# Block attention with a top-1 MoE on one core: six router operations as scalar_tensor_tensor, and a new order of steps in nine plan strings

## The chip, the cores and the metric

The kernel runs on one core of a Trainium2 chip. Its time is the device time of one execution in microseconds; the median of three runs before the change is 945.31 us (942.5 to 946.25). The engines are TensorE (PE, with its weight loads shown apart as PEld), VectorE (DVE), ScalarE (ACT), GpSimd (POOL) and SyncE (SP, which here only issues DMAs).

## What is computed

Attention over 8 batches of 8 heads, 576 positions of 64 values, where a query sees the blocks of 64 keys up to its own; then its output, 4608 tokens of 512 values, goes through a mixture of 8 experts of which each token takes one.

```python
def _attn_ref(q, k, v):
    scores = scale * np.matmul(q, k.transpose(0, 1, 3, 2))
    mask = block_i >= block_j                     # blocks of 64
    scores = np.where(mask, scores, -1000000000.0)
    scores = scores - np.max(scores, axis=-1, keepdims=True)
    attn = np.exp(scores)
    attn = attn / (np.sum(attn, axis=-1, keepdims=True) + 1e-09)
    return np.matmul(attn, v)

def _moe_ref(x, expert_emb, tau, w1, w2):
    xn = x / (np.linalg.norm(x, axis=-1, keepdims=True) + 1e-06)
    en = expert_emb / (np.linalg.norm(expert_emb, axis=-1, keepdims=True) + 1e-06)
    logits = xn @ en.T / tau
    expert_idx = np.argmax(logits, axis=1)
    probs = np.exp(logits - logits.max(-1, keepdims=True))
    probs /= probs.sum(-1, keepdims=True) + 1e-09
    gate_w = probs[np.arange(N), expert_idx]
    for e in range(E):                            # 512 -> 1024 -> 512
        h = np.maximum(x[expert_idx == e] @ w1[e], 0.0)
        out[expert_idx == e] = gate_w[...] * (h @ w2[e])
```

## The kernel before

**Attention.** A loop of 32 iterations, n = 0 to 31, handles one pair of heads each: batch b = n // 4, pair n % 4. An iteration works on four pairs at once, in stages: the scores of n, the row maxima of n+1, the transposes and casts of n+2, the values and the finish of n-1, and the loads of n+3. Each stage is a Python generator that writes its instructions up to a `yield`, one step at a time. A **plan string** says which generator takes its next step, letter by letter, and so sets the order in which every engine's queue is written:

- `s`, scores(n), 10 steps of which five belong to each head: two matmuls on PE (L366 and L367, of 288, 288, 448, 320, and 192 + 64 columns), the exponential on ACT (L376, L383), and for the last three of five an addition to the row sums' tile pS on POOL (L357, `add`).
- `m`, maxes(n+1), 12 steps: 11 with a matmul (L336) into psm (two buffers) and a reduction on DVE (L337), then one that turns the maxima (L342), copies them on ACT (nmT, L344) and sends them with two SP DMAs to qx.
- `v`, values(n-1), 9 steps: six of value matmuls on PE (L396) into psb, a copy of them on ACT (oe, L402), the row sums and the router's products on PE (L411, L414) into the same psb, and their copy on ACT (su, L416).
- `f`, finish(n-1), 4 steps: transposes of su and oe on PE into psb (L426, L428); the reciprocals and the scaled rows on DVE (L433 to L437); the router's logits on DVE (L440, L443); the end, at which the fourth pair of a batch puts that batch's router on the list `slow`.
- `p`, prep(n+2), 6 steps: transposes of q and k on PE (L295), casts on ACT (L307, L311, L316), low parts on DVE (L286), copies within SBUF by SP DMAs (L309, L319).
- `l`, the loads of n+3: seven SP DMAs.
- `r`, one step of the oldest router on `slow`, nothing when there is none. The router of a batch, route(b), is some 45 small operations on DVE, five squares on ACT, a power on POOL (L538), ranks on PE into psm (L496 to L500), the store of the rows, and five scatters into a table in DRAM, which are indirect DMAs issued by POOL (L560). The last router but one ends with `early_rows`: index arithmetic on POOL (L576 to L580) and two gathers (L591) of tokens for the first expert.
- `k`, in iteration 0 alone, a part of the router's set-up.

PLAN0 is for n = 0, the first four strings of PLANS for n % 4 = 0, 1, 2, 3, and the last four for n = 28 to 31. Letters that are missing are drained at the iteration's end. psb has one buffer, so finish(n-1) waits for ACT's copy of the sums, and values(n) in the next iteration wait for the last read of finish(n-1) on DVE (L443). An engine runs its queue in the order written, and waits where an operand isn't there.

**After the loop** the list `slow` is drained, the first expert's weights are split into high and low parts (L741, L745), the two gathered tiles are turned on PE (L927), the values, the finish and the router of the last pair run between the first expert matmuls (L940), and the other slots follow one after another to the end.

Of the kernel before, what the change touches and what calls it, by code (L numbers as in the profile page):

```python
# [8 lines left out]
F32 = mybir.dt.float32  # L9
# [4 lines left out]
ALU = mybir.AluOpType  # L14
# [16 lines left out]
PLAN0 = "smkmmmskspmmmrmmsmpkrspmsssslpspp"


@with_exitstack
def kernel(
# [30 lines left out]
    const = ctx.enter_context(tc.tile_pool(name="const", bufs=1))  # L66
# [96 lines left out]
    def pool(stack, name, bufs, **kw):  # L163
        return stack.enter_context(tc.tile_pool(name=name, bufs=bufs, **kw))
# [8 lines left out]
    op = pool(left, "op", 1)  # L173
# [290 lines left out]
    def bc(ap, *shape):  # L464
        return ap.to_broadcast(shape)

    def route(b, xrow, lgh, ssp):

        lg = sm.tile([P, NJ, E], F32, name="lg")
# [5 lines left out]
        nc.vector.tensor_scalar(lg, lg, itau, None, op0=ALU.mult)
# [32 lines left out]
        nc.vector.tensor_tensor(acc, acc, oa, op=ALU.add)
        yield
        if b == B - 1:  # L510
            nc.vector.tensor_tensor(accb, acc, early, op=ALU.subtract)
        else:
            nc.vector.tensor_copy(accb, acc)
# [16 lines left out]
        ss = sm.tile([P, NJ], F32, name="ss")  # L530
        gs = sm.tile([P, NJ], F32, name="gs")
# [10 lines left out]
        nc.vector.tensor_scalar(ss, ss, 1.0e-6, None, op0=ALU.add)
# [3 lines left out]
        nc.vector.tensor_tensor(lg, lg, bc(ss.unsqueeze(2), P, NJ, E), op=ALU.mult)
# [149 lines left out]
    for n in range(NPAIR):  # L696
# [613 lines left out]
```

## Time and profile before

| | |
|---|---|
| median of three runs | 945.31 us |
| the profiled execution | 943.41 us |
| its span | 941.6 us |
| mean granted clock of TensorE | 0.964 |
| attention's loop, from the first value matmul to the end of n = 31 | 34.1 to about 466 us |
| a batch (four iterations), n = 5 to 8 | 55.1 us |
| a batch, n = 21 to 24 | 58.0 us |

A row of the timeline reads: start in us, duration, engine, line, operation, output<-inputs with their shapes, xcount where equal neighbours are drawn together, and in brackets how long the engine stood before it and what ended that. A row of the windows reads: stretch and width, busy time of PE, PEld, DVE, ACT and POOL with the number of instructions, then the granted clock, the share of the DMA engines, and GB/s. A row of a group by lines ends with its total and the mean in ns, then the idle time before.

### The profile page before, as it was taken

To read this page: it belongs to the slowest core of one execution; us is meant where nothing else is said; L and a number is where in the kernel's file an instruction comes from. 1 tells how busy PE (TensorE), PEld (TensorE's weight loads), DVE (VectorE), ACT (ScalarE), POOL (GpSimd) and SP (SyncE) were. 2 spreads that over 40 slices of the span, in tenths; PEclk is the share of its full clock that TensorE was granted. 3 is DMA by queue.
4 is the path that set the end of the run, shared out by engine and by line. 5 is a ranking of instruction groups with operands and counts; after the bars stand their busy time and mean duration, and the time that the engine had idled before them with its cause. 6 is when DMAs were issued, how large, how long until landed. Compare 5 with 4: busy or idle time off the path is not lost. (4 is left out here: it accounts for less than half of the span.)

```text
span 941.6 us, 20617 instructions
## 1 busy us (share of the span) xinstructions
PE 878.1 (93%) x5609; PEld 673.8 (72%) x5609; DVE 681.6 (72%) x1602; ACT 486.9 (52%) x1028; POOL 447.2 (47%) x483
## 2 busy tenths in 40 slices
PE   5999989898998989998688999999999999999997
PEld 4676666667666666666466788777888888888886
DVE  7577868686785867757377488767777888888882
ACT  3565757476575755746555453545444332253222
POOL 5344554646454463544743074687747211173111
PEclk9999999999997989979789899999999999999999
DMA  7766867576684756845345444464535211111111
GB/s 148 158 140 142 197 129 154 138 150 158 139 197 105 158 138 129 200 104 165 126 171 186 176 146 136 136 203 143 185 101 185 85 47 47 47 43 47 47 42 45
DMA packets 155175, 122.29 MB, mean 130 GB/s; under 512 B 122217, under 2 KB 123513, under 8 KB 155020
## 3 DMA queue, kind: packets, MB, share of 16 engines
q1 hardware_dynamic: 147372, 100.14, 42.9%
q0 software_dynamic: 7648, 20.44, 6.8%
q8 instruction: 54, 0.88, 0.4%
q14 instruction: 101, 0.83, 0.3%
HBM read 72.71 MB, written 19.71 MB: 98 GB/s over the span
## 5 line engine op out<-in xcount | busy, mean ns | idle before, releaser
L986 DVE STREAM_TRANSPOSE pt<-h 32x256 f32<-32x256 f32 x528 | 240.8, 456 | 18.5 <-ACT h L958 0.5
L337 DVE TENSOR_REDUCE nmx<-psm 128x1 f32<-128x320 f32 x315 | 136.8, 454 | 88.3 <-PE psm L336 76.6
L376 ACT ACTIVATE pT<-pss 128x448 f32<-128x448 f32 (+1 forms) x254 | 110.1, 452 | 103.0 <-PE pss L367 95.6
L745 POOL TENSOR_TENSOR ring_l<-raw,ring_h 128x1024 f32 (+1 forms) x52 | 123.7, 2408 | 41.1 <-ACT ring_h L741 40.3
L357 POOL TENSOR_TENSOR pS<-pS,pT 128x320 f32<-128x320 f32 (+2 forms) x192 | 115.3, 600 | 54.1 <-ACT pT L376 25.8
L357 POOL TENSOR_TENSOR pS<-pT 128x448 f32<-128x448 f32 x64 | 73.0, 1140 | 142.8 <-ACT pT L376 142.7
L366 PE MATMUL pss<-qb,ka 128*128 128x448 f32 (+1 forms) x382 | 129.0, 349 | 7.6 <-ACT pT L376 4.7
L1000 POOL DMA_INDIRECT out_dram<-y,outi x36 | 36.0, 1001 | 197.7 <-ACTq L894 142.3
L336 PE MATMUL psm<-kd,qd 128*128 128x320 f32 x315 | 105.2, 368 | 18.9 <-DVE nmx L337 12.3
L367 PE MATMUL pss<-qx,kx 70*128 70x448 f32 (+1 forms) x382 | 115.2, 322 | 3.4 <-DMA qx<-nmT 2.2
L940 PE MATMUL py<-ring_h,hh 128*128 (+1 forms) x280 | 113.0, 404 | 2.6 <-ACT hh L992 2.6
L396 PE MATMUL psb<-pT,vo 128*64 128x64 f32 (+4 forms) x768 | 113.9, 422 | 0.0
L940 PE MATMUL py<-ring_h,hl 128*128 (+1 forms) x280 | 112.1, 400 | 1.1 <-DVE hl L994 1.0
L940 PE MATMUL ph<-ring_h,xh 128*128 x280 | 110.3, 394 | 0.5 <-issue 0.5
L940 PE MATMUL ph<-ring_l,xh 128*128 x280 | 110.0, 393 | 0.5 <-POOLq L906 0.5
L940 PE MATMUL ph<-ring_h,xl 128*128 x280 | 110.0, 393 | 0.0
L940 PE MATMUL py<-ring_l,hh 128*128 (+1 forms) x280 | 109.8, 392 | 0.0
L336 PEld LDWEIGHTS psm<-kd,qd 128*128 128x128 f32 x315 | 59.2, 199 | 65.1 <-DVE nmx L337 36.0
L366 PEld LDWEIGHTS pss<-qb,ka 128*128 128x128 f32 x382 | 78.2, 205 | 26.2 <-ACT pT L376 10.9
L958 ACT ACTIVATE h<-ph 128x512 f32<-128x512 f32 x70 | 41.9, 599 | 93.6 <-DVE pt L986 74.8
L994 DVE TENSOR_TENSOR hl<-pt,hh 128x512 fp32r<-128x512 f32 x66 | 42.5, 686 | 63.7 <-ACT hh L992 61.5
L367 PEld LDWEIGHTS pss<-qx,kx 70*128 70x128 f32 x382 | 79.0, 207 | 5.1 <-issue 4.1
(262 smaller groups left out, 1578.9 us busy)
## 6 DMA issues: line engine op xcount, KB each, us to landing
raw<-in_moe_w_dram SPq DMA_DIRECT2D x64, 512.0 KB
ka<-kd SPq DMA_DIRECT2D x128, 144.0 KB
qn<-in_q_dram SPq DMA_DIRECT2D x64, 144.0 KB
kn<-in_k_dram SPq DMA_DIRECT2D x64, 144.0 KB
qx<-qb SPq DMA_DIRECT2D x32, 288.0 KB
vo<-in_v_dram SPq DMA_DIRECT2D x64, 128.0 KB
xbuf<-xrow SPq DMA_DIRECT2D x7, 1040.0 KB
qx<-nmT SPq DMA_DIRECT2D x64, 2.2 KB
```

The lines of the kernel that those rows point to most:

```text
L336: nc.tensor.matmul(mx[:, 0:e - a], qd[d][:, j, :, :], kd[d][:, a:e], start=True, stop=True)
L337: nc.vector.tensor_reduce(m[:, j + u:j + u + 1], mx[:, 0:e - a], axis=AX.X, op=ALU.max, negate=True)
L357: nc.gpsimd.tensor_tensor(o, pT[0:r, P:S] if t == 1 else o, pT[0:r, off[t]:off[t] + w], op=ALU.add)
L366: nc.tensor.matmul(o, ka[i][:, hh, ts], qb[i][:, hh, c0:c1], start=True, stop=False)
L367: nc.tensor.matmul(o, kx[i][0:KX, hh, ts], qx[i][0:KX, hh, c0:c1], start=False, stop=True)
L376: nc.scalar.activation(pT[:, o:o + c1 - c0], st[:, 0:c1 - c0], AF.Exp, scale=scale)
L396: nc.tensor.matmul(ob[hh * D:(hh + 1) * D, c0:c1], a[:, t, hh, :], pTs[hh][0][:, o:o + c1 - c0], start=(t == 0), stop=(c0 == 448 or t == N ...
L745: return eng.tensor_tensor(piece(ring_l, to, c, half), raw[i][:, c * CW:(c + 1) * CW], piece(ring_h, to, c, half).bitcast(F32), op=ALU.sub ...
L940: m = nc.tensor.matmul(out, ac, w, start=(c == 0 and w is wh and a is sh), stop=(c == nk - 1 and a is sl_))
L958: nc.scalar.activation(h[:, f:f + 512], ph, AF.Relu)
L986: nc.vector.transpose(pt[32 * j:32 * j + 32, :, 32 * i:32 * i + 32], h[32 * i:32 * i + 32, :, j, :])
L994: nc.vector.tensor_tensor(sets["hl"][u], pt[:, 4 * u:4 * u + 4], sets["hh"][u].bitcast(F32), op=ALU.subtract)
```

## The change

Six DVE operations of the router become scalar_tensor_tensor, four of them with a new tile of zeros, zeroj, or a slice of it as the second tensor; each computes what it computed. zeroj is one more memset ahead of the loop. All nine plan strings are written anew; the letters of the stages are the same in number, but for `r`, of which many now fall where no router is pending and do nothing. Lines behind L121 move by two, so L357 before is L359 after.

```diff
 PLANS = (
-    "rrrvvsmmrvmsrrvmsvrvvmrmpmrrsvvrprsmrsrlmrrmfrrmmrpfsfrpssrfsrrprp",
-    "mvrvrvvmrmrvmvsmmvssrpsmsrrvrvssprpmmfmlsfmfprfrmsrpsrp",
-    "mrrvvrrrmvmmvvvmvmsspmssvrvrlrpsmsrmmfpffrmsspfrspmrrprsrrrr",
-    "rvvrrrrrvvrmrrsmrrrsrmrspmmvvrvrrsrmmprvrmmrrrrvrssmfmrrprsmrrlfrsprrsrsfprrfp",
+    "rrrrrvrrvrvvvvmsmsvmrrmsrsrmrrprrrrmsmrrrsrrrmvrrrrrrrvrsrsrprrrpmrrmfrrrrrrfrrrrrrrrmlfrrfsprsrrrprmp",
+    "vvvvvvmrsmsrvmsmsmpmsmsrmvvpspmsmfmflprfrmprrrrsrsrfp",
+    "vvvvvvvmssmrmsmpmsmsvvpmmssmmfpmsrflfmrrppsrpsf",
+    "rvvrvssmrmrsrsrrmrpmrvvvvprmmrrrvvmsmpsmfrrrrrmfffsrsmlpsrrsmrrpprr",
...
-    "rrvrrvrrvvrmrrsmrsrrrrmrspmmvmrvrrsrmvprvrrrmmrvrssmfmrprsmrrfrslprsrsrfrrfpp",
+    "vlmrvmrvprrrpvvmvpvmspsmmrmrmvmrrrmmvssprpfsfsfmfssss",
 )
...
+    zeroj = const.tile([P, NJ, E], F32, name="zeroj")
+    nc.vector.memset(zeroj, 0.0)
...
-        nc.vector.tensor_scalar(lg, lg, itau, None, op0=ALU.mult)
+        nc.vector.scalar_tensor_tensor(lg, lg, itau, zeroj, op0=ALU.mult, op1=ALU.add)
...
-        nc.vector.tensor_tensor(acc, acc, oa, op=ALU.add)
+        nc.vector.scalar_tensor_tensor(acc, oa, 1.0, acc, op0=ALU.mult, op1=ALU.add)
...
-            nc.vector.tensor_copy(accb, acc)
+            nc.vector.scalar_tensor_tensor(accb, acc, 1.0, zeroj[:, 0], op0=ALU.mult, op1=ALU.add)
...
-        nc.vector.tensor_scalar(ss, ss, 1.0e-6, None, op0=ALU.add)
+        nc.vector.scalar_tensor_tensor(ss, ss, 1.0e-6, zeroj[:, :, 0], op0=ALU.add, op1=ALU.add)
...
-        nc.vector.tensor_tensor(lg, lg, bc(ss.unsqueeze(2), P, NJ, E), op=ALU.mult)
+        nc.vector.scalar_tensor_tensor(lg, lg, 1.0, bc(ss.unsqueeze(2), P, NJ, E), op0=ALU.mult, op1=ALU.mult)
...
-        nc.vector.tensor_scalar(gs, gs, 1.0e-9, None, op0=ALU.add)
+        nc.vector.scalar_tensor_tensor(gs, gs, 1.0e-9, zeroj[:, :, 0], op0=ALU.add, op1=ALU.add)
```

Where the order changes, three places are shown. The first is POOL's queue around the five scatters of a batch; L357 (L359 after) is the addition to pS, in the sizes 448, 320, 192 and 64 for each head of a pair. Before:

```order
L357 TENSOR_TENSOR pS<-pT 128x448
L357 TENSOR_TENSOR pS<-pS,pT 128x320
L357 TENSOR_TENSOR pS<-pS,pT 128x192
L357 TENSOR_TENSOR pS<-pS,pT 64x64
L560 DMA table<-tokf,rowj 36864x1 x5
L357 TENSOR_TENSOR pS<-pT 128x448
```

The five scatters stood together between two iterations' additions. After, at the same place of a batch, in iteration n % 4 = 3:

```order
L359 TENSOR_TENSOR pS<-pT 128x448
L359 TENSOR_TENSOR pS<-pS,pT 128x320
L562 DMA table<-tokf,rowj 36864x1
L359 TENSOR_TENSOR pS<-pS,pT 128x192
L359 TENSOR_TENSOR pS<-pS,pT 64x64
L562 DMA table<-tokf,rowj 36864x1 x4
L359 TENSOR_TENSOR pS<-pT 128x448
```

The scatters moved behind the first head's additions, the first of them ahead of the last two.

The second place is PE from the transposes of a finish to the first value matmul of the next iteration, at the end of n = 4 (n % 4 = 0). psb is the shared buffer, L342 turns the maxima, L295 transposes k, L366 and L367 are scores. Before:

```order
L428 MATMUL psb<-ident,oe_194 128x128 x5
L342 MATMUL psm<-ident,nmx_192 9x128
L366 MATMUL pss<-qb_176,ka_182 128x288
L367 MATMUL pss<-qx_179,kx_185 128x288
L295 MATMUL pst<-ident,kn 128x96 x6
L366 MATMUL pss<-qb_176,ka_182 128x448
L367 MATMUL pss<-qx_179,kx_185 128x448
L366 MATMUL pss<-qb_176,ka_182 128x320
L367 MATMUL pss<-qx_179,kx_185 128x320
L366 MATMUL pss<-qb_176,ka_182 128x192
L367 MATMUL pss<-qx_179,kx_185 128x192
L366 MATMUL pss<-qb_176,ka_182 128x64
```

One more score matmul and one of maxima followed, then the first value matmul. After, from the same transposes on:

```order
L344 MATMUL psm<-ident,nmx_194 9x128
L368 MATMUL pss<-qb_178,ka_184 128x320
L369 MATMUL pss<-qx_181,kx_187 128x320
L297 MATMUL pst<-ident,kn 128x96 x6
L368 MATMUL pss<-qb_178,ka_184 128x192
L369 MATMUL pss<-qx_181,kx_187 128x192
L368 MATMUL pss<-qb_178,ka_184 128x64
L369 MATMUL pss<-qx_181,kx_187 128x64
L398 MATMUL psb<-pT,vo_161 64x64 x2
L398 MATMUL psb<-pT,vo_161 64x512 x2
L398 MATMUL psb<-pT,vo_161 64x448 x2
L398 MATMUL psb<-pT,vo_161 64x320 x2
```

The score steps of 288 and 448 columns and the maxima no longer stand between, and the value steps follow each other, six in a row, before the first of the maxima.

The third place is POOL at the end of the loop, n = 31, around the two gathers ex. Before:

```order
L357 TENSOR_TENSOR pS<-pT 128x448
L357 TENSOR_TENSOR pS<-pS,pT 128x320
L576 CAST ei<-et 128x2
...
L580 CAST ei<-enone 128x2
L591 DMA ex_202<-xbuf,ei 128x520
L591 DMA ex_203<-xbuf,ei 128x520
L357 TENSOR_TENSOR pS<-pS,pT 128x192
L357 TENSOR_TENSOR pS<-pS,pT 64x64
L357 TENSOR_TENSOR pS<-pT 128x448
L357 TENSOR_TENSOR pS<-pS,pT 128x320
```

Two further additions followed. After, all eight additions stand ahead:

```order
L359 TENSOR_TENSOR pS<-pT 128x448
L359 TENSOR_TENSOR pS<-pS,pT 128x320
L359 TENSOR_TENSOR pS<-pS,pT 128x192
L359 TENSOR_TENSOR pS<-pS,pT 64x64
L578 CAST ei<-et 128x2
...
L582 CAST ei<-enone 128x2
L593 DMA ex_204<-xbuf,ei 128x520
L593 DMA ex_205<-xbuf,ei 128x520
L747 TENSOR_TENSOR ring_l_6399<-raw_124,ring_h_6398 128x1024
```

The gathers moved behind the last six additions of the loop, and behind them POOL goes on with the weights' low parts.

More of the change, by code (lines that the diff above doesn't have):

```diff
@@ L21 @@
 PLANS = (
-    "rrrvvsmmrvmsrrvmsvrvvmrmpmrrsvvrprsmrsrlmrrmfrrmmrpfsfrpssrfsrrprp",
-    "mvrvrvvmrmrvmvsmmvssrpsmsrrvrvssprpmmfmlsfmfprfrmsrpsrp",
-    "mrrvvrrrmvmmvvvmvmsspmssvrvrlrpsmsrmmfpffrmsspfrspmrrprsrrrr",
-    "rvvrrrrrvvrmrrsmrrrsrmrspmmvvrvrrsrmmprvrmmrrrrvrssmfmrrprsmrrlfrsprrsrsfprrfp",
-    "rrrvvmsmrvmsrrvmmsvrvvmrpmrrrsvvprsmrsrlrrmmfrrmmrpfspfsrsrfsrrprp",
-    "rmvvrvrvvvmvmmrsmmssrpsmsrrrvvssprpmmfmlsfmfprsfrmprsrp",
-    "mmvrrrvvrmvssprmmvvmvmssvrvrmrlrpsmsmfpffrmsrspsfrpmrrprsrrrr",
-    "rrvrrvrrvvrmrrsmrsrrrrmrspmmvmrvrrsrmvprvrrrmmrvrssmfmrprsmrrfrslprsrsrfrrfpp",
+    "rrrrrvrrvrvvvvmsmsvmrrmsrsrmrrprrrrmsmrrrsrrrmvrrrrrrrvrsrsrprrrpmrrmfrrrrrrfrrrrrrrrmlfrrfsprsrrrprmp",
+    "vvvvvvmrsmsrvmsmsmpmsmsrmvvpspmsmfmflprfrmprrrrsrsrfp",
+    "vvvvvvvmssmrmsmpmsmsvvpmmssmmfpmsrflfmrrppsrpsf",
+    "rvvrvssmrmrsrsrrmrpmrvvvvprmmrrrvvmsmpsmfrrrrrmfffsrsmlpsrrsmrrpprr",
+    "vvvvrvvmmssmrvmsrsrmpmsmsrmvvrpsprmsmfmflffrppssmrp",
+    "vvvrvmrmrssmsmsmrpmrmvrvvmsspmmvprvmsrrlspmrfrsfsfppf",
+    "rrmprrrspvvrvvmmsrsvrmmsrsmmlmvvsrmsmrrvvrprprsspfsmrffrrprfmr",
+    "vlmrvmrvprrrpvvmvpvmspsmmrmrmvmrrrmmvssprpfsfsfmfssss",
 )
-PLAN0 = "smkmmmskspmmmrmmsmpkrspmsssslpspp"
+PLAN0 = "rmsmssrrrmrrrrrrrkrrrsrmsrsrrrrmmrrrsrrrmrrrrpsrrrmrmmrrmrlprsrprrrrrrkrprsrrrrpkrrrp"
 @with_exitstack
```

## The prediction

> **What bounds the kernel now.** I read the page first, then windows cut at the iterations' borders (from one first value matmul to the next), then the timeline inside them.
>
> ```profile
> span 941.6 us, 20617 instructions
> ...
> PE 878.1 (93%) x5609; PEld 673.8 (72%) x5609; DVE 681.6 (72%) x1602; ACT 486.9 (52%) x1028; POOL 447.2 (47%) x483
> ...
> PEclk9999999999997989979789899999999999999999
> ```
>
> TensorE is busy for 93% of the span, and its clock is below full in a few slices of the first half only. The windows below are the iterations n = 5, 6, 7 and 8, then n = 19 and 20, and the MoE's stretch: width, busy time of PE, PEld, DVE, ACT, POOL, granted clock, DMA share, GB/s.
>
> ```profile
> 85.20:98.10 12.90, 12.43 (x117) 8.94 (x116) 11.16 (x32) 7.72 (x18) 6.16 (x10) 1.00 0.63 133
> 98.10:110.50 12.40, 12.00 (x110) 8.72 (x109) 9.87 (x29) 10.91 (x29) 6.54 (x10) 1.00 0.87 170
> 110.50:126.80 16.30, 13.48 (x111) 10.39 (x110) 10.35 (x27) 8.24 (x20) 10.83 (x14) 0.90 0.46 130
> 126.80:140.30 13.50, 12.96 (x113) 8.87 (x111) 10.11 (x23) 8.70 (x21) 6.06 (x9) 1.00 0.89 181
> 275.50:292.90 17.40, 14.43 (x111) 11.23 (x110) 10.76 (x28) 8.71 (x21) 11.39 (x14) 0.80 0.44 124
> 292.90:307.90 15.00, 14.46 (x112) 9.49 (x111) 9.63 (x23) 8.41 (x19) 5.42 (x8) 0.89 0.78 160
> 530.00:941.00 411.00, 401.70 (x1820) 326.61 (x1818) 311.94 (x645) 166.36 (x290) 183.17 (x118) 1.00 0.32 102
> ```
>
> The MoE has 401.7 us of PE in 411 us and isn't touched by the change: it stays. What can move is the attention half. Four kinds of iteration with the same matmuls of attention take 12.9, 12.4, 16.3 and 13.5 us. Iteration n%4 = 3 is the odd one: PE stands for 2.8 of its 16.3 us, POOL is at 10.8 us instead of 6, and the clock falls to 0.90. The timeline says why:
>
> ```profile
> 114.38 1.12 POOL L560 DMA_INDIRECT table<-tokf,rowj  x1 [0.57 <-DVE nmx L337]
> ...
> 119.65 0.97 POOL L560 DMA_INDIRECT table<-tokf,rowj  x1 [0.30 <-issue]
> ...
> 121.77 0.32 ACT L416 COPY su<-psb 128x192 f32<-128x192 f32 x1 [2.33 <-PE pss L367]
> 121.80 0.56 DVE L337 TENSOR_REDUCE nmx<-psm 128x1 f32<-128x192 f32 x2 [2.62 <-PE pss L367]
> ...
> 122.21 0.42 PE L336 MATMUL psm<-kd,qd 128*128 128x64 f32 x1 [1.52 <-DVE nmx L337]
> ...
> 122.00:124.00 2.00, 1.79 (x9) 1.72 (x10) 1.34 (x4) 0.68 (x3) 1.62 (x3) 0.55 0.00 0
> ...
> 294.00:296.00 2.00, 2.00 (x8) 0.97 (x4) 0.00 (x0) 0.02 (x1) 0.74 (x2) 0.50 1.23 229
> ```
>
> POOL issues the route's five scatters back to back from 114.38 to 119.65 us. ACT and DVE then stand for 2.33 and 2.62 us and PE for 1.52 us, although what they wait for is long done, and all three go on at about 121.8 us, 2.1 us behind the last scatter. After that the granted clock is 0.55, and in the late batches still 0.50 at 294 us, inside the next iteration: that is why n = 20 takes 15.0 us and n = 8 takes 13.5.
>
> **The plan strings, inside a batch.** All nine strings write the same steps in another order. Four places matter.
>
> *The scatters.* In the old n%4 = 3 string they lie among the first letters. In the new one the first scatter comes before the values' copy, and the other four stand on POOL behind the additions of the fifth score step. PE's work ahead of that step is all values and sums, seven of eleven maxes and half of the scores, some two thirds of an iteration of 12.9 us; I estimate 8.7 us. Four scatters 1.32 us apart (5.27 us for four gaps above) and the 2.1 us until all goes on make 6.1 us, so the blocked end falls 13 to 15 us into the iteration: at its seam with the next one, which in the new strings opens with six value steps in a row.
>
> ```profile
> 110.52 2.49 PE L396 MATMUL psb<-pT,vo 128*64 128x64 f32 x16
> ...
> 139.53 0.36 PE L366 MATMUL pss<-qb,ka 128*128 128x192 f32 x1 [0.44 <-ACT pT L376]
> ```
>
> Four such steps took 2.49 us, six some 3.2 us. They read probabilities that ACT made long before and need only the free buffer psb, so PE has work that waits for nothing new during its 1.52 us. I take those 1.52 us as gone in the six batches that have this stall (n = 7 to 27): **−9 us**. Bounds: 0, if the stall finds another uncovered place; and, if the clock drop goes with it, both iterations at 12.9 and 13.5 us: 3.4 us in three early batches and 4.5 + 1.5 = 6.0 us in three late ones, −28 us.
>
> *The crowded end of n%4 = 0.* The old string leaves its scores s8, s9 and s10 to the last eight letters, among ACT's casts; PE waits 0.44 us for ACT there (row above). The new string writes s7 and s8 right behind the values. I take its 13.5 us to 12.8, between its neighbours' 12.4 and 12.9 us: 0.7 × 7 = **−4.9 us** (bounds 0 and −1.1 × 7 = −7.7).
>
> *The loop through psb.* One psb buffer carries values, sums and finish in turn, so an iteration's first value matmul waits for the DVE chain of the finish before it:
>
> ```profile
> 149.61 0.71 PE L428 MATMUL psb<-ident,oe 128*128 128x128 f32 x5
> ...
> 150.75 0.30 PE L336 MATMUL psm<-kd,qd 128*128 128x64 f32 x1 [0.43 <-DVE nmx L337]
> ...
> 151.22 0.15 DVE L433 TENSOR_SCALAR rin<-psb 128x8 f32<-128x8 f32 x1
> ...
> 151.73 0.82 DVE L437 TENSOR_TENSOR xrow<-psb,rin 128x640 f32<-128x640 f32 x1
> ...
> 152.60 0.16 DVE L443 TENSOR_TENSOR lgh<-psb,rin 128x16 f32<-128x16 f32 x1
> ...
> 153.23 0.77 PE L396 MATMUL psb<-pT,vo 128*64 128x64 f32 x6
> ```
>
> The transposes end at 150.32, the chain at 152.76 us: 2.44 us, of which some 0.3 us is queueing behind a max, so about 2.1 us are needed. PE had work until 153.23 here and never waited for psb. From 150.75 to 153.23 that is 2.48 us of PE, 12 rows. The new order leaves fewer steps between; each at its share of these 2.48 us, I estimate 1.4 us (n%4 = 0), 1.7 (1), 1.9 (2) and 2.4 (3). If all of the difference to 2.1 us were lost, that is 0.7 + 0.4 + 0.2 = 1.3 us a batch, +9 us in seven; to the 2.44 us of this place, 1.0 + 0.7 + 0.5 + 0.1 = 2.3 us, +16 us. I don't take all of it: PE's busy time for the same matmuls is 12.00 us at n = 6 and 12.96 at n = 8, so an iteration holds up to a microsecond of waiting inside busy rows, and matmuls moved from the seam to another place fill that. I take +0.3 us a batch: **+2.1 us** (bounds 0 and +16).
>
> *SP's queue.* The regular strings now put the loads behind the maxima's two small DMAs; three of the four old ones had them ahead. The loads are for n + 3 and have two iterations until they are used; I cost it at nothing. If that cover were gone, prep would wait for a load that it has never waited for in the trace.
>
> **The six router operations.** Rows per line: count, then shortest, median and longest in ns.
>
> ```profile
> L475 DVE TENSOR_SCALAR lg<-lg,itau x8: 742/750/1893, 84.8 to 485.7; 128x40 f32<-128x40 f32 x8
> ...
> L546 DVE TENSOR_TENSOR lg<-lg,ss x8: 193/196/201, 111.9 to 492.1; 128x40 f32<-128x40 f32 x8
> ...
> L508 DVE TENSOR_TENSOR acc<-acc,oa x8: 166/690/694, 93.7 to 489.7; 128x8 f32<-128x8 f32 x8
> ...
> L513 DVE CAST accb<-acc x7: 658/685/694, 97.6 to 437.0; 128x8 bf16<-128x8 f32 x7
> ...
> L542 DVE TENSOR_SCALAR ss<-ss x8: 164/894/896, 110.3 to 491.6; 128x5 f32<-128x5 f32 x8
> ...
> L626 DVE SCALAR_TENSOR_TENSOR row<-rowj,row x7: 165/165/709, 105.1 to 451.0; 128x5 f32<-128x5 int32 x7
> ...
> 450.82 0.88 POOL L357 TENSOR_TENSOR pS<-pS,pT 128x320 f32<-128x320 f32 x1
> 451.02 0.71 DVE L626 SCALAR_TENSOR_TENSOR row<-rowj,row 128x5 f32<-128x5 int32 x1
> ```
>
> Operations of 8 to 40 elements take 0.69 to 0.89 us in the median and 0.16 to 0.20 when free. The excess is 750 − 196, 690 − 166, about 685 − 166 and 894 − 164 ns: 2.3 us of DVE a batch, 16 us in seven. But DVE is busy 11.16 us of 12.9 at most, so this is cover time on DVE, not time on the path. Only L508's excess stands right ahead of a PE wait, the 0.43 us at 150.75. And the one scalar_tensor_tensor in the trace that met a POOL addition waited it out: begun 0.20 us into the addition, it took 0.71 us and ended with it. So I take the new form to wait as the old does: **0 us**, bounds −0.5 × 7 = −3.6 (no wait at all) and +1 (zeroj's memset, and two-operand reads).
>
> The Trainium skill speaks against this part of the change: its page "SBUF — State Buffer", section "SBUF: two separate sides", says that VectorE and GpSimd share a pair of ports as an exclusive lock, which a VectorE operation takes in a two-port mode, or with two inputs in SBUF against a GpSimd operation that reads SBUF. The new forms with zeroj or acc have two SBUF inputs, so by that rule nothing is saved, and L626's 709 ns agrees; if the form were exempt, the sum would be lower by the −3.6 us above.
>
> **Into the MoE.** In the new n = 31 string the last batch's gathers fall out of the iteration and are drained after the loop, behind all of POOL's additions.
>
> ```profile
> 464.85 1.10 POOL L591 DMA_INDIRECT ex<-xbuf,ei  x1 [0.62 <-issue]
> ...
> 470.79 1.12 PE L927 MATMUL pe<-ident,ex 128*128 128x128 f32 x4 [2.76 <-DMA ex<-xbuf,ei]
> ...
> 472.89 1.11 PE L927 MATMUL pe<-ident,ex 128*128 128x128 f32 x4 [0.98 <-DMA ex<-xbuf,ei]
> ...
> L357 POOL TENSOR_TENSOR pS<-pT 128x448 f32<-128x448 f32 x59 | 67.3, 1140 | 136.0 <-ACT pT L376 135.9
> L357 POOL TENSOR_TENSOR pS<-pS,pT 128x320 f32<-128x320 f32 x59 | 51.1, 866 | 25.5 <-ACT pT L376 22.9
> L357 POOL TENSOR_TENSOR pS<-pS,pT 128x192 f32<-128x192 f32 x59 | 35.0, 594 | 18.8 <-ACT pT L383 16.1
> L357 POOL TENSOR_TENSOR pS<-pS,pT 64x64 f32<-64x64 f32 x59 | 18.5, 314 | 4.6
> ```
>
> PE already waits for both gathers (2.76 and 0.98 us). Six additions now stand ahead of them: 2 × 0.594 + 2 × 0.314 + 1.140 + 0.866 = 3.8 us, if the iteration is otherwise as long. PE has value steps for some of it. I take **+3.5 us**, bounds 0 (n = 31 ends as much earlier) and +6. The first iteration's string and the other steps of the last batch: 0 ± 3.
>
> **Sum.** −9 − 4.9 + 2.1 + 0 + 3.5 = −8.3 us on the profiled execution's 943.4 us (its span of 941.6 and 1.8 around it): **935 us**. That execution is 1.9 us below the median of the three runs, 945.3; a measurement of this kernel tells about 0.5% (4.7 us) from no change.
>
> **Rivals.** *The psb loop becomes the bound* (slower): each iteration begins with value matmuls that wait for the finish. For it: the 2.1 us against 1.4 us, and a PE that waits nowhere else at the seam. Against it: the microsecond of slack inside an iteration. It decides where PE's work between the transposes and the first value matmul is below 2.1 us and the stall is not covered either: 943.4 + 16 + 3.5 = 963 us. *The stall only moves* (no change): the blocked engines hold the new seam's finish, and so psb itself; then the −9 us are 0, and the rest (−4.9 + 2.1 + 3.5) about cancels: 944 us. For it: it is DVE that stands longest, 2.62 us. *The clock drop goes too* (much faster): −28 instead of −9, 935 − 19 = 916 us, or 910 with the six operations exempt and n%4 = 0 at its bound (−3.6 and −2.8). For it: the drop follows PE's idle stretch. Against it: 1.5 us was enough to cause it. The Trainium skill's page "TensorE: Matmul & The Clock Gate", section "What's actually happening", gives the half clock only after an idle window of about 3.4 us; the trace disagrees, since 1.52 us of idleness stood ahead of 0.55, and with the rule alone there would be no drop to lose. *The new form doesn't wait* is the rival on what the change says: 935 − 3.6 = 931 us; L626 speaks against it, one row of seven, and I count it inside the forecast.
>
> **How the numbers follow.** Forecast 0.37, clock drop gone 0.15, no change 0.20, psb loop 0.28. The range leaves a tenth at each end: from 910 (the bound with all gains) to 962 us, the psb rival's full price but one. The forecast's own range is 929 to 940 us. Faster by over 0.5%: 0.52; within: 0.20; slower: 0.28.
>
> **What would show it.** Windows by iteration: n%4 = 3 at about 14.5 to 15 us with PE idle under 1 us, n%4 = 0 at 12.8 us. In the timeline, six L398 steps running while ACT and DVE stand after the scatters; the clock rows still at 0.5. The first L398 step of n%4 = 2 with an idle of 0.3 us named for DVE lgh. L510 and L544 with medians as before or wherever POOL runs, since the lock stays. The first PE L929 transposes later behind the gathers by 3 to 4 us. I am wrong if the scatters leave the engines standing as long as now, if the first value step waits for lgh in every iteration by 0.5 us or more, or if the clock column shows 1.00 throughout.

## The result and the profile after

The changed kernel takes **891.70 us** (median of 4 runs, 888.24 to 893.86) where the kernel before takes 945.53 us on the same chip: a ratio of 0.9433 with a 95% interval of 0.9396 to 0.947. The prediction was 935 us with a range of 910 to 962; the time lies below the range. The profiled execution takes 891.42 us, 52.0 us less than the one before.

The page of the changed kernel, the three lines that were shown of the kernel before:

```profile
span 889.7 us, 20632 instructions
...
PE 837.6 (94%) x5609; PEld 669.2 (75%) x5609; DVE 675.3 (76%) x1603; ACT 481.5 (54%) x1028; POOL 448.5 (50%) x483
...
PEclk9999999999999999995999999999999999999999
```

The same matmuls keep PE busy for 837.6 us instead of 878.1, and the granted clock is below full in one slice only, the one at the end of the loop. The windows of the changed kernel for the iterations n = 5, 6, 7, 8, and 19 and 20 (columns as in the prediction):

```profile
79.80:91.50 11.70, 11.59 (x118) 9.51 (x119) 10.69 (x31) 8.09 (x19) 5.58 (x8) 1.00 0.66 153
91.50:103.20 11.70, 11.61 (x112) 9.29 (x112) 10.06 (x25) 10.28 (x28) 5.64 (x10) 1.00 0.67 155
103.20:115.00 11.80, 11.56 (x110) 8.82 (x110) 11.03 (x33) 8.62 (x21) 8.58 (x12) 1.00 0.86 222
115.00:127.90 12.90, 11.62 (x113) 9.41 (x113) 8.96 (x22) 8.07 (x20) 9.99 (x13) 1.00 0.71 168
248.80:260.70 11.90, 11.57 (x112) 8.86 (x112) 11.09 (x34) 8.73 (x21) 8.57 (x12) 1.00 0.86 222
260.70:273.50 12.80, 11.31 (x111) 9.32 (x111) 8.89 (x22) 7.95 (x19) 9.90 (x13) 1.00 0.71 167
```

Three of the four kinds of iteration now take 11.7 to 11.9 us, and the fourth 12.9. The clock is 1.00 in all of them, early and late. Only n = 11 is longer than its kind (13.1 us; the reason is in the section on the prediction). Summed over the trace, cut at the first value matmul of each iteration:

| stretch | before, us | after, us | difference |
|---|---|---|---|
| start to the first value matmul | 34.1 | 31.5 | −2.6 |
| n = 1 to 4 | 51.1 | 48.3 | −2.8 |
| n%4 = 1, six of n = 5 to 28 | 77.5 | 69.9 | −7.6 |
| n%4 = 2, six | 74.5 | 70.4 | −4.1 |
| n%4 = 3, six | 101.1 | 72.4 | −28.7 |
| n%4 = 0, six | 85.4 | 77.4 | −8.0 |
| n = 29 to 31 | 42.2 | 41.5 | −0.7 |
| after the loop | 475.8 | 478.2 | +2.4 |

In iterations n = 3 and 4 no router is pending, so no scatters run in them or just before, and they show what the order of the other steps does alone. The kernel before, then the changed kernel:

```profile
59.90:71.70 11.80, 11.54 (x111) 8.80 (x110) 8.86 (x21) 8.15 (x19) 5.83 (x9) 1.00 0.35 78
71.70:85.20 13.50, 12.96 (x113) 8.88 (x112) 10.13 (x23) 8.66 (x20) 6.06 (x9) 1.00 0.88 181
```

```profile
56.30:68.10 11.80, 11.53 (x110) 8.76 (x111) 8.96 (x22) 7.93 (x19) 5.76 (x9) 1.00 0.66 152
68.10:79.80 11.70, 11.26 (x110) 9.34 (x111) 8.93 (x22) 8.01 (x19) 6.41 (x10) 1.00 0.66 153
```

The new order of steps leaves n%4 = 3 at 11.8 us and brings n%4 = 0 from 13.5 to 11.7. With these as the times without a stall, the stall of the scatters, waits and clock together, cost 34.7 us in the twelve iterations n%4 = 3 and 0 before the change and 8.7 us after it (1.2 of these are n = 11's). So an estimated 26 us of the gain are the stall's, and about 25 us come from the order of the other steps: 10.7 in n%4 = 0, 7.6 and 4.1 in n%4 = 1 and 2, and 2.8 in n = 1 to 4. It is an estimate, as n = 3 and 4 have none of the router's other operations either.

What became of the stall is in the timeline of the changed kernel at the seam of n = 7 and n = 8:

```profile
113.57 1.02 POOL L562 DMA_INDIRECT table<-tokf,rowj  x1 [0.39 <-issue]
...
115.04 2.93 PE L398 MATMUL psb<-pT,vo 128*64 128x64 f32 x24
...
117.47 0.98 POOL L562 DMA_INDIRECT table<-tokf,rowj  x1 [0.30 <-issue]
...
117.89 0.41 PE L338 MATMUL psm<-kd,qd 128*128 128x320 f32 x1
...
118.53 0.37 PE L369 MATMUL pss<-qx,kx 70*128 70x288 f32 x1
...
119.48 0.82 DVE L339 TENSOR_REDUCE nmx<-psm 128x1 f32<-128x320 f32 x2 [2.92 <-PE pss L369]
119.61 0.71 ACT L378 ACTIVATE pT<-pss 128x288 f32<-128x288 f32 x2 [3.98 <-PE pss L369]
...
120.03 0.80 PE L338 MATMUL psm<-kd,qd 128*128 128x512 f32 x2 [0.74 <-DVE nmx L339]
```

The scatters hold ACT and DVE as before: the first max is done at 118.30 us and the first score at 118.90, but DVE and ACT take them up at 119.48 and 119.61, 2.0 us behind the start of the last scatter. Held are 1.2 and 0.7 us; the rest of the 2.92 and 3.98 us in brackets is the time in which PE runs values and makes nothing for them. PE runs its 24 value matmuls from 115.04 to 117.97 us, then two maxes and two scores, and stands for 0.74 us only. In the six batches that wait is 0.35 to 1.16 us, and no clock drop follows any of them.

The seventh batch's scatters run in n = 31 in both kernels. In the changed kernel PE is busy there for 1.06 of the 3 us from 400 to 403 us, and the granted clock is 0.50 from 403.0 to 426.9 us: that is the slice below full, and a stall that the change left.

### The profile page after: what moved, and what is told of

The parts are those of the page before. It is cut to its first block, busy times and chain, and to the rows that moved or that the text cites. A ratio compares the mean times of both kernels' runs of the same rounds, so it can differ in the third digit from the quotient of the medians.

```text
span 889.7 us, 20632 instructions
## 1 busy us (share of the span) xinstructions
PE 837.6 (94%) x5609; PEld 669.2 (75%) x5609; DVE 675.3 (76%) x1603; ACT 481.5 (54%) x1028; POOL 448.5 (50%) x483
## 5 line engine op out<-in xcount | busy, mean ns | idle before, releaser
L378 ACT ACTIVATE pT<-pss 128x448 f32<-128x448 f32 (+1 forms) x254 | 107.3, 449 | 86.3 <-PE pss L369 64.6
L359 POOL TENSOR_TENSOR pS<-pS,pT 128x320 f32<-128x320 f32 (+2 forms) x192 | 114.8, 598 | 44.3 <-ACT pT L385 17.7
L359 POOL TENSOR_TENSOR pS<-pT 128x448 f32<-128x448 f32 x64 | 73.4, 1146 | 113.4 <-ACT pT L378 113.4
L368 PE MATMUL pss<-qb,ka 128*128 128x448 f32 (+1 forms) x382 | 119.7, 325 | 1.4 <-ACT pT L378 1.2
L369 PE MATMUL pss<-qx,kx 70*128 70x448 f32 (+1 forms) x382 | 110.2, 312 | 1.0 <-issue 0.6
L398 PE MATMUL psb<-pT,vo 128*64 128x64 f32 (+4 forms) x768 | 100.0, 405 | 6.3 <-DVE lgh L445 3.7
L398 PEld LDWEIGHTS psb<-pT,vo 128*64 128x64 f32 x768 | 52.5, 140 | 46.7 <-issue 32.1
L1001 ACT ACTIVATE y<-py,xg 128x512 f32<-128x512 f32 x35 | 24.1, 689 | 112.9 <-PE py L942 112.9
L368 PEld LDWEIGHTS pss<-qb,ka 128*128 128x128 f32 x382 | 74.7, 196 | 13.8 <-issue 4.9
```

The costliest lines, as they stand in the source:

```text
L359: nc.gpsimd.tensor_tensor(o, pT[0:r, P:S] if t == 1 else o, pT[0:r, off[t]:off[t] + w], op=ALU.add)
L368: nc.tensor.matmul(o, ka[i][:, hh, ts], qb[i][:, hh, c0:c1], start=True, stop=False)
L369: nc.tensor.matmul(o, kx[i][0:KX, hh, ts], qx[i][0:KX, hh, c0:c1], start=False, stop=True)
L378: nc.scalar.activation(pT[:, o:o + c1 - c0], st[:, 0:c1 - c0], AF.Exp, scale=scale)
L398: nc.tensor.matmul(ob[hh * D:(hh + 1) * D, c0:c1], a[:, t, hh, :], pTs[hh][0][:, o:o + c1 - c0], start=(t == 0), stop=(c0 == 448 or t == N ...
```

## The experiments

The kernels ran in three groups of four, each group on one chip with the kernel before beside it. Its medians there were 942.05 us (e1 to e4), 909.49 us (f1 to f4) and 943.65 us (g1 to g4), so a time is compared within its group, and iterations by their windows. A plan string's edit is given as its steps, in which s1 is the first step of scores, and names in angle brackets are the router's (ind0 to ind4 are the scatters).

**The two halves apart.** e1 has the new operations under the old strings, e2 the new strings with the old operations.

```diff
 e1: PLANS and PLAN0 as before; the six operations as after
 e2: PLANS and PLAN0 as after; the six operations as before
```

> The six operations as scalar_tensor_tensor under the old plan strings. Order theory (the new strings alone made the gain; the new form waits for a running POOL addition as the old did): 945 us, within 3 us of the kernel before, and the six operations keep medians of 0.65 to 0.9 us wherever they begin during an addition. Rival (the new form doesn't wait, and DVE was the hidden bound): medians of 0.15 to 0.26 us, 16 us of DVE time gone, and 930 us or less.

> The new plan strings with the six operations in their old form. Order theory: 892 us, within 4 us of the changed kernel. Rival (the operations carry part of it): above 897 us.

e1: 941.26 us, ratio to the kernel before 0.9995 (0.9948 to 1.0043). e2: 894.87 us, ratio 0.9482 (0.9416 to 0.9548). So the strings carry the gain, and the operations nothing that can be told from zero within half a per cent. Two of the operations in e1, by line (shortest, median, longest in ns):

```profile
L510 DVE SCALAR_TENSOR_TENSOR acc<-oa,acc x8: 166/685/699, 93.7 to 494.5; 128x8 f32<-128x8 f32 x8
...
L544 DVE SCALAR_TENSOR_TENSOR ss<-ss,zeroj x8: 161/890/894, 110.2 to 496.4; 128x5 f32<-128x5 f32 x8
```

They take what the old forms took, since the order puts them against the same POOL additions. In the changed kernel the order moved them, and the medians with it:

```profile
L510 DVE SCALAR_TENSOR_TENSOR acc<-oa,acc x8: 167/855/877, 92.3 to 439.4; 128x8 f32<-128x8 f32 x8
...
L544 DVE SCALAR_TENSOR_TENSOR ss<-ss,zeroj x8: 154/154/169, 107.1 to 441.3; 128x5 f32<-128x5 f32 x8
...
140.28 1.55 POOL L359 TENSOR_TENSOR pS<-pS,pT 128x320 f32<-128x320 f32 x2 [0.50 <-ACT pT L378]
140.31 0.86 DVE L510 SCALAR_TENSOR_TENSOR acc<-oa,acc 128x8 f32<-128x8 f32 x1
```

L544 fell into a gap of POOL and takes 154 ns; L510 begins 0.03 us into an addition and waits nearly all of it out, longer than before. What the prediction expected of the new form, that it waits as the old one does, is what these rows show.

**The scatters early again, in the new order.** e3 moves only router letters of two strings.

```diff
 n%4 = 2:
- ... s8 <sq5> f2 L f3 m12 <pow> <tr1> p4 p5 s9 <tr2> p6 s10 f4
+ ... v8 <tr3> v9 <tr4> ... s10 <geps> <grec> f4 <store> <ind0>
 n%4 = 3:
- <tr3> v1 v2 <tr4> v3 ... <store> <ind0> v8 v9 ... f1 <ind1> <ind2> <ind3> <ind4> m10 ...
+ <ind1> v1 v2 <ind2> <ind3> <ind4> v3 ... v8 v9 ... f1 m10 ...
```

> The changed kernel with the router's letters moved in two of the regular strings (n%4 = 2 and 3), so that the five scatters are issued at the start of n%4 = 3 again; the order of all other steps is the new one. Cover theory (what counts is that six value steps lie over the end of the scatters): the iteration n%4 = 3 goes from 11.9 back to 14.5 to 17 us with the clock at 0.8 to 0.9 there, +20 to +35 us, 912 to 927 us. Rival (the gain is that of the attention steps' order, wherever the scatters lie): 890 to 897 us, the clock at 1.00.

927.74 us, ratio 0.9862 (0.9794 to 0.9929), 33 us above e2 in the same group. The windows of n = 7 and n = 8 of e3, and the scatters with the wait behind them:

```profile
105.30:122.90 17.60, 13.91 (x112) 11.04 (x112) 9.89 (x27) 8.02 (x20) 10.53 (x14) 0.81 0.64 170
122.90:134.60 11.70, 11.27 (x113) 9.14 (x113) 8.98 (x22) 8.11 (x20) 6.53 (x10) 1.00 0.67 154
...
108.74 1.12 POOL L562 DMA_INDIRECT table<-tokf,rowj  x1 [0.58 <-DVE nmx L339]
...
114.02 0.97 POOL L562 DMA_INDIRECT table<-tokf,rowj  x1 [0.30 <-issue]
...
115.50 0.42 PE L413 MATMUL psb<-pT,ones 128*32 128x128 f32 x1 [3.67 <-ACT oe L404]
```

PE stands for 3.67 us in mid-iteration and the clock falls: the iteration is back at 17.6 us, in the new order of steps. So the place of the scatters decides 27 us (n%4 = 3 in six batches takes 104.0 us against 72.0 in e2, n%4 = 0 73.1 against 78.1); the router's letters moved into n%4 = 2 cost another 8 (78.4 against 70.3 us), and all other stretches together gain 2.6. The expectation held. In two of the six batches the half clock reaches into n%4 = 0 (13.1 and 13.2 us; 11.7 in the other four).

**The scatters late, in the old order.** e4 gives the kernel before the new place of the scatters and six value steps in a row at n%4 = 0.

```diff
 n%4 = 2: the last letter, <ind0>, goes
 n%4 = 3:
- <ind1> v1 v2 <ind2> <ind3> <ind4> v3 v4 ... p2 v8 ... m10 f1 m11 ...
+ v1 v2 v3 v4 ... p2 <ind0> v8 ... m10 f1 <ind1> <ind2> <ind3> <ind4> m11 ...
 n%4 = 0:
- v1 v2 s1 m1 m2 v3 m3 s2 v4 m4 s3 v5 v6 v7 ...
+ v1 v2 v3 v4 v5 v6 s1 m1 m2 m3 s2 m4 s3 v7 ...
```

> The kernel before with the scatters moved to the new place (the first ahead of the values' copy, four behind step 1 of finish, in n%4 = 3) and with the first six value steps of n%4 = 0 in a row; all else in the old order. Cover theory: the stall and the clock drop go, n%4 = 3 at 12.5 to 13.5 us and n%4 = 0 at 13 to 14 us in all batches, -25 to -36 us, 909 to 920 us. Rival (the new steps' order is needed as a whole): 935 to 945 us.

932.05 us, ratio 0.9896 (0.9869 to 0.9923): a third of what was expected. The windows of n = 11, 12 and 16 of e4, and the seam of 11 and 12:

```profile
163.70:175.80 12.10, 11.62 (x113) 8.81 (x112) 10.22 (x28) 8.38 (x20) 7.33 (x10) 1.00 0.61 175
175.80:194.90 19.10, 16.61 (x114) 13.14 (x113) 10.94 (x26) 8.69 (x20) 9.57 (x12) 0.73 0.70 142
232.30:247.60 15.30, 12.50 (x114) 9.22 (x113) 10.21 (x23) 8.43 (x20) 9.59 (x12) 1.00 0.74 157
...
175.78 2.92 PE L396 MATMUL psb<-pT,vo 128*64 128x64 f32 x24
...
178.63 0.98 POOL L560 DMA_INDIRECT table<-tokf,rowj  x1 [0.30 <-issue]
...
181.36 0.50 PE L336 MATMUL psm<-kd,qd 128*128 128x512 f32 x1 [1.93 <-DVE nmx L337]
```

n%4 = 3 lost its stall as foreseen (12.1 us), but the last scatter is issued 2.85 us behind the seam, against 2.43 us in the changed kernel, and only one score step lies between the value run and the max that waits, where the new order has two. PE stands for 1.93 us where 0.74 were left there. Four of the six stalls then bring the clock drop (n = 12: 0.73), two don't (n = 16: 15.3 us at 1.00, with a wait of 1.89 us). The traces show what parts them: in all of them the granted clock changes only at the borders of a grid of 3.41 us (in e4 half clock begins at 128.24, 182.85 and 292.08 us, 16 and 32 such steps apart). Two neighbouring stretches of the grid at n = 12, then two at n = 16:

```profile
179.44:182.85 3.41, 1.49 (x7) 1.13 (x7) 1.75 (x5) 0.90 (x3) 3.11 (x5) 1.00 0.54 112
182.86:186.26 3.40, 3.17 (x23) 2.48 (x26) 1.86 (x4) 2.19 (x4) 1.13 (x1) 0.50 0.68 160
...
234.05:237.46 3.41, 1.89 (x18) 1.32 (x14) 0.17 (x1) 0.15 (x1) 3.02 (x4) 1.00 1.13 226
237.47:240.88 3.41, 2.69 (x16) 2.10 (x17) 3.05 (x7) 1.75 (x5) 2.68 (x4) 1.00 0.75 176
```

At n = 12 the wait lies in one stretch, of which PE is busy for 1.49 us, and the next has half the clock. At n = 16 a border cuts the wait into 1.52 and 0.37 us, and the clock stays. So the cover has to reach to the end but for about a microsecond, and above that the place on the grid decides.

**The value run cut at the seam.** f3 leaves the scatters where the change put them and cuts only the opening of n%4 = 0.

```diff
- v1 v2 v3 v4 v5 v6 m1 s1 m2 s2 v7 m3 ...
+ v1 v2 s1 m1 m2 v3 m3 s2 v4 v5 v6 v7 ...
```

> The changed kernel with the first six value steps of n%4 = 0 no longer in a row but cut by scores and maxes as in the old string (v1 v2 s1 m1 m2 v3 m3 s2 v4 v5 v6); nothing else moves, the scatters neither. Cover theory: PE meets a max that waits for DVE before the updates come back and stands for 1.5 to 3 us, the clock drop returns in most batches, n%4 = 0 at 14 to 17 us, +10 to +28 us. Rival (place of the scatters alone counts): n%4 = 0 within 0.5 us of 12.85.

900.13 us in a single run, in the group where the kernel before took 909.49. The windows of n = 4 (no scatters before it), 8 and 12 of f3, and what PE stood for in n = 8:

```profile
68.10:80.20 12.10, 11.67 (x110) 8.97 (x111) 9.07 (x22) 8.17 (x19) 6.38 (x10) 1.00 0.65 148
115.50:131.30 15.80, 13.33 (x110) 9.43 (x110) 8.99 (x22) 8.09 (x19) 9.80 (x13) 0.89 0.58 136
167.80:181.30 13.50, 11.86 (x112) 9.03 (x113) 9.14 (x22) 8.23 (x19) 9.93 (x13) 1.00 0.69 164
...
119.06 0.37 PE L369 MATMUL pss<-qx,kx 70*128 70x288 f32 x1 [2.08 <-DMA qx<-nmT]
```

Without scatters the cut costs 0.4 us (12.1 against 11.7). Behind scatters it costs 1.5 us without a clock drop and 3.8 with one in these two rows, against f4 on the same chip, where the uncut opening takes 12.0 us. The cover theory held, but the drop came in three of the six batches and not in most: behind waits of 1.97, 2.08 and 2.46 us, and not behind those of 1.00 to 1.28 us. What PE waited for was not a max, as expected, but the SP transfer of the row maxima that the first score reads.

**Values in a row, or maxes and scores in turn.** f4 makes two edits, read apart by iteration.

```diff
 n%4 = 1:
- v1 v2 v3 v4 v5 v6 m1 s1 m2 s2 v7 m3 ...
+ v1 v2 m1 v3 s1 v4 m2 v5 s2 v6 v7 m3 ...
 n%4 = 2:
- v7 m1 s1 s2 m2 m3 s3 m4 p1 m5 s4 m6 s5 v8 ...
+ v7 m1 m2 m3 m4 s1 s2 s3 s4 p1 m5 m6 s5 v8 ...
```

> The changed kernel with two unlike edits, read by iteration: in n%4 = 1 the first six value steps are cut by m1, s1, m2 and s2 (five cuts); in n%4 = 2 the steps of maxes and scores, alternating before, come two to four of a kind in a row. Theory A (the steady gain comes from values in a row): n%4 = 1 goes from 11.65 to 12.1 us or more, n%4 = 2 stays within 0.15 of 11.72. Theory B (it comes from alternating, since two maxes in a row wait for DVE and two scores for ACT): n%4 = 2 goes to 12.2 us or more, n%4 = 1 stays below 11.9.

```profile
82.30:95.20 12.90, 12.76 (x118) 9.08 (x119) 10.86 (x31) 8.27 (x19) 5.57 (x8) 1.00 0.61 139
95.20:108.10 12.90, 11.92 (x112) 9.30 (x112) 9.97 (x25) 10.39 (x28) 5.74 (x10) 1.00 0.61 140
```

Both effects are there, and with the same price: n%4 = 1 and n%4 = 2 (above, n = 5 and 6 of f4) go from 11.7 to 12.9 us each. They look different. The cut values leave PE busy for 12.76 of 12.9 us: the time is inside the rows. The start of n = 9 in the timeline of f4:

```profile
131.93 1.20 PE L398 MATMUL psb<-pT,vo 128*64 128x64 f32 x8 [0.43 <-DVE lgh L445]
133.06 0.42 PE L338 MATMUL psm<-kd,qd 128*128 128x320 f32 x1
133.40 0.97 PE L398 MATMUL psb<-pT,vo 128*64 128x448 f32 x4
```

And where the changed kernel goes from a max to a score:

```profile
130.73 0.42 PE L338 MATMUL psm<-kd,qd 128*128 128x320 f32 x1
130.98 0.29 PE L368 MATMUL pss<-qb,ka 128*128 128x288 f32 x1
```

The same max is followed by a value matmul after 0.34 us in f4 and by a score after 0.25 us here. A value matmul fills 64 of the array's columns (128*64), and those of the two heads run side by side; a max or a score takes all 128. The four steps written between the values make eight more changes from the one to the other on PE than the block that they came from (v7 is a copy on ACT), and cost 1.2 us: some 0.15 us a change, with no idle time in front of any row. The rows of the value matmuls alone tell the same at full clock: they are busy for 2.93 us where they stand in one piece (n = 4 to 6 of the changed kernel), 3.15 in two (n = 3 of both kernels), 3.36 to 3.38 in three (n = 5 and 6 before), 3.59 in four (n = 4 before) and 3.81 in five (n = 5 of f4). That the half width is the reason was not tested. The maxes in a row show as waits instead: at n = 6 of f4 0.47 us for DVE, then 0.29 us for ACT.

```profile
99.03 0.80 PE L338 MATMUL psm<-kd,qd 128*128 128x512 f32 x2 [0.47 <-DVE nmx L339]
...
100.65 0.47 PE L368 MATMUL pss<-qb,ka 128*128 128x448 f32 x1 [0.29 <-ACT pT L378]
```

**Can the stall be made smaller still?** f1 spreads the four later scatters behind score steps 5, 8, 9 and 10; f2 puts the second scatter beside the first.

```diff
 f1: ... <ind0> v8 v9 m7 s5 <ind1> m8 p3 s6 m9 f1 ... s8 <ind2> m11 L p4 s9 <ind3> s10 <ind4> ...
 f2: ... <ind0> <ind1> v8 v9 m7 s5 ... f1 <ind2> <ind3> <ind4> ...
```

> The changed kernel with the four later scatters apart on POOL: behind the additions of score steps 5, 8, 9 and 10 of n%4 = 3, one each. Theory that the stall comes from several scatters under way at once: no engine stands behind them for over 1 us, n%4 = 0 goes from 12.85 to about 11.8 us, 883 to 887 us. Rival (each scatter holds the others' progress for its own 1.3 us, wherever it is): the waits add up in other places and end later than the value run, n%4 = 0 and 3 together 25 to 28 us instead of 24.7, 892 us or more, with the clock drop back in some batches.

> The changed kernel with the second scatter right behind the first, ahead of the values' copy, so that three instead of four are issued together and the last is out some 1.3 us earlier. Cover theory: PE's wait in n%4 = 0 (0.74 us) goes since the value run now covers the whole end; n%4 = 0 about 12.1 us, 886 to 889 us. Rival: the two early scatters stall n%4 = 3 itself, which goes to 12.5 us or more, 891 us or more.

881.77 and 880.98 us, ratios 0.9691 (0.967 to 0.9712) and 0.9678 (0.9642 to 0.9713) to a kernel before that took 909.49 us there. n%4 = 0 comes to 11.7 to 12.5 us in both. The expected times were set against the changed kernel, which wasn't run on that chip; so neither is told apart from its rival by the time. But f4 left n%4 = 3 and 0 as the change wrote them, and its six iterations n%4 = 0 take 71.7 us together, those of f1 and f2 71.7 and 71.4: on this chip neither edit brought anything there. f1's edit is in g3 below, with the changed kernel beside it on another chip.

**The gathers, and all together.** g4 moves the gathers of n = 31 ahead of the last four score steps, and so of the loop's last four additions. g3 has that edit, the spread scatters of f1, and the value steps v1 to v7 in a row in n = 29 and 30. g1 and g2 are the changed kernel and the kernel before again.

```diff
 n = 31 (g3, g4):
- ... p6 f1 s5 f2 s6 f3 m12 f4 s7 s8 s9 s10
+ ... p6 f1 <et> <12 waits> s5 f2 s6 f3 m12 f4 <eidx> <ein0> <ein1> s7 s8 s9 s10
```

> The changed kernel itself, to stand beside the three others on one chip. In two calls the kernel before took 942 and 909 us, so chips differ. If they differ in how long the scatters hold the engines' progress, the change gains less where the kernel before is fast: with a kernel before of about 942 us this is 890 to 895 us, with one of about 909 us it is 880 to 888 us, and n%4 = 1 and 2 take 11.65 and 11.72 us in both. If the chips differ in the clock or in everything, those two iterations differ as well.

> The kernel before itself, for its trace on the same chip. Theory as in g1: iterations n%4 = 1, 2 and 0 (without a clock drop) take 12.9, 12.4 and 13.5 us as ever, and only n%4 = 3 (12.1 us of work) and the clock behind it differ between chips: 16.3 to 17.7 us with 942 us in all, 14 to 15 us and few clock drops with 909 us.

> The changed kernel with the scatters spread as in f1, the seven value steps in a row in n = 29 and 30 as well, and the two gathers ahead of the last two score steps of n = 31. Sum of parts: spread -2 to -7 us, the two iterations -0.5 each, gathers -3 to -5 us: 7 to 13 us below the changed kernel on the same chip. Rival: the spread scatters were worth nothing beside the changed kernel on this chip, and POOL's additions behind the gathers make the last sums late: within 3 us of the changed kernel.

> The changed kernel with one edit, the router's letters of n = 31: the index arithmetic and the two gathers stand on POOL ahead of the last head's last five additions. If the gathers' place is the whole loss at the transition: PE's wait for the gathered tiles (7.8 us) falls to 1 to 4 us and the time by 3 to 5 us against the changed kernel on the same chip. Rival (the expert matmuls wait for the last weights' parts or the router anyway): the wait falls and the time stays within 1.5 us.

| kernel | median, us | ratio to the kernel before (943.65) |
|---|---|---|
| g1, the changed kernel | 894.24 | 0.945 (0.9391 to 0.9509) |
| g2, the kernel before, a single run | 941.01 | |
| g4 | 890.47 | 0.9424 (0.9368 to 0.9481) |
| g3 | 883.17 | 0.9335 (0.9276 to 0.9395) |

g4 is 3.8 us below g1. The wait for the gathered tiles, in the changed kernel and in g4:

```profile
421.56 2.06 PE L929 MATMUL pe<-ident,ex 128*128 128x128 f32 x8 [7.83 <-DMA ex<-xbuf,ei]
```

```profile
418.30 2.10 PE L929 MATMUL pe<-ident,ex 128*128 128x128 f32 x8 [4.27 <-DMA ex<-xbuf,ei]
```

3.6 us of wait went, and as much of the time. g3 is 11 us below g1 and the fastest beside the changed kernel. Of it n%4 = 0 has 7.0 us (six iterations: 78.0 to 71.0 us in the two traces), the stretch behind the loop 4.6; the value steps of n = 29 and 30 brought nothing (25.2 us against 25.1). g2 repeats the trace of the kernel before, stalls and clock drops included. The expectation that the chips differ in the stall alone could not be tested, as the kernel before wasn't traced on the chip where it took 909 us.

## Why the prediction was wrong

The direction was right and the size was not: −8 us were forecast, −52 measured. Two terms were far too small, the stall by some 17 us and the order of the other steps by some 22 us.

- **The scatters: the mechanism was right, the term was mis-sized.** The prediction took "those 1.52 us as gone in the six batches", −9 us, and kept the clock drop. The step that failed is this price: the idle time of one row. All waits and the clock together cost an estimated 34.7 us, measured against n = 3 and 4 of the same trace, and 26 of them went. The rival *the clock drop goes too*, at a chance of 0.15, was the true one for this term, and its −28 us nearly its size. The cover itself was placed less well than thought: the blocked end was put 13 to 15 us into the iteration, and it comes at 16.3 us (119.48 in the rows of the result), 1.5 us behind the value run. The two maxes and two scores that follow the run, which the prediction did not count, cover the rest but for 0.35 to 1.16 us. As e4 shows, not much more would have brought the drop back, so that it went in all six batches is in part luck. e3 and f3 show the cause from both sides: with the scatters moved back the stall and the drop return, with the values moved back the stall does, and the drop in half of the batches.
- **The steady iterations: a term was left out.** For n%4 = 1 and 2 the sum had nothing but the seam's +0.3 us. They lost 7.6 and 4.1 us, and n = 1 to 4 another 2.8. The step that failed is the reading that the four kinds differ through their ends ("the crowded end of n%4 = 0") and that the slack "inside busy rows" is only a cushion. f4 shows two things that fill iterations: value steps cut by full-width matmuls, and maxes in a row that wait for DVE. Both stood in the old strings. Their value matmuls came in four, three, three and two pieces (n%4 = 0, 1, 2, 3) and come in one, one, one and two now; without scatters the iterations gain 1.8, 1.3, 0.7 and 0 us, in that order. A piece more costs 0.2 to 0.3 us (two more in f3 0.4 us, four more in f4 1.2 us), so the pieces make up about half of the gain. How the rest divides was not measured. The page had a sign of it, in the group of the value matmuls; before and after:

```profile
L396 PE MATMUL psb<-pT,vo 128*64 128x64 f32 (+4 forms) x768 | 113.9, 422 | 0.0
```

```profile
L398 PE MATMUL psb<-pT,vo 128*64 128x64 f32 (+4 forms) x768 | 100.0, 405 | 6.3 <-DVE lgh L445 3.7
```

  The same 768 matmuls went from 113.9 to 100.0 us, the clock's share and the overlap with the rows behind each piece included. A row with no idle time in front was taken for a row at its floor.
- **The crowded end of n%4 = 0:** −4.9 us forecast, to 12.8 us; it is at 12.9 in the mean, but for another reason. Where no scatters stand in front (n = 4) it takes 11.7 us, and the stall's remainder makes up the rest.
- **The psb loop:** +2.1 us forecast. The row above has 3.7 us of PE waiting for DVE lgh ahead of value steps, in nine places: the term was about right, and the slower rival with its +16 us fell with it. The place was not: 0.43 us stand at the start of n%4 = 1, where n%4 = 2 had been named.
- **The six operations:** 0 forecast; e1 measured a ratio of 0.9995. The Trainium skill's rule ("SBUF — State Buffer", section "SBUF: two separate sides"), that an operation with two SBUF inputs waits for a GpSimd operation that reads SBUF, agrees with L510's 855 ns.
- **Into the MoE:** +3.5 us forecast, +2.4 measured behind the loop and 0.6 in n = 31. PE's waits for the gathered tiles grew from 2.76 and 0.98 us to 7.83, and g4 takes 3.8 us back by moving the gathers alone.
- **SP's queue:** 0 forecast, and a load that prep waits for was named as the sign that the cover is gone. It shows once in the loop of the changed kernel, in n = 11:

```profile
156.61 0.69 PE L297 MATMUL pst<-ident,qn 96*128 96x96 f32 x6 [1.04 <-DMA qn<-in_q_dram]
```

  All other traces of the new order have such a wait in n = 11 too, of 0.31 to 1.04 us, and none of the old order has it. It costs one iteration 1.2 us.
- **The first iteration:** 0 ± 3 forecast; the start is 2.6 us shorter, within the bound. The change of PLAN0 was not run by itself.

## What to carry to other kernels

When an engine's progress is held from outside (here by scatters), look for the longest stretch of work that waits for nothing new and put it over the end of the hold, with a margin: waits of 0.4 to 1.3 us at the seam left the clock alone here, waits of 1.75 us and more cost it in seven of nine batches (e4 and f3). Put matmuls of half the array's width in one run, and let steps that wait for different engines alternate. Price a stall by what follows from it, the clock too, and not by the idle time of one row; an iteration without the stall, which the trace may already hold, gives that price.

## What the runs showed of the hardware

- Behind four scatters issued together DVE and ACT take up finished operands 1.2 and 0.7 us late, and go on 2.0 us behind the start of the last scatter; in the kernel before, with five, 2.1 us behind it. Neither has a part in the scatters. Behind a single one (ind0 of the changed kernel, at 109.81 us) the longest waits of PE and ACT until the next are 0.22 and 0.76 us. What holds them back was not settled.
- The clock drop is not decided by the length of one wait. In all 14 traces the granted clock changes at borders of a 3.41 us grid only. In attention (from 35 us to 20 us before the loop's end) every stretch of the grid in which PE stood for less than 1.07 us is followed by full clock, every one with more than 1.53 us by half; in between it goes either way. Several short waits do it too: from 398.67 to 402.08 us of the kernel before PE is busy for 1.93 of 3.41 us, no wait is longer than 0.48 us, and the clock falls. By the Trainium skill's "TensorE: Matmul & The Clock Gate", section "What's actually happening", the window is free-running, which fits that; its 3.4 us of idleness do not, since less than half of it was enough here.
- The gain seems to depend on the chip. The kernel before took 942, 909 and 944 us in the three groups, while n%4 = 1 and 2 in the new order took 11.65 and 11.72 us in traces of all three. On the chip with 909 us n%4 = 0, as the change wrote it, takes 11.9 to 12.0 us (f4) against 12.8 to 13.2 on the others, and at n = 8 DVE goes on 0.9 us behind the last scatter, as soon as the max is there. f1 and f2, whose edits brought nothing in n%4 = 0 there, take 28 us less than the kernel before; that is an estimate of what the change itself is worth on that chip, against 49 to 54 us on two others. It is near the 25 us of the order of steps, as if little stall were left to cover, but the kernel before was not traced there.
